# Softmax denominators in four strips of 32 columns instead of two of 64

## The chip, the core and the metric

The kernel runs on one NeuronCore of a Trainium2 chip, a core with five engines that each work through a queue of their own: TensorE (PE, matmuls into PSUM; its weight loads are listed apart as PEld), VectorE (DVE), ScalarE (ACT), GpSimd (POOL) and SyncE (SP, which here only issues DMAs). An instruction that waits holds up what stands behind it in the same queue. The metric is the device time of one execution in microseconds; lower is better.

## What is computed

Attention in which a query sees only the keys of its own cluster, followed by a bilinear feed-forward block. Four batches, 8 heads, 768 tokens, head dimension 64; 512 model columns, 1536 hidden columns; all float32.

```python
q_assign = np.argmax(np.einsum('bhsd,hcd->bhsc', q_n, c_n), axis=-1)
k_assign = np.argmax(np.einsum('bhsd,hcd->bhsc', k_n, c_n), axis=-1)
mask = q_assign[:, :, :, None] == k_assign[:, :, None, :]
scores = np.where(mask, scale * np.matmul(q, k.transpose(0, 1, 3, 2)), -1e9)
attn = np.exp(scores - np.max(scores, axis=-1, keepdims=True))
attn = attn / (np.sum(attn, axis=-1, keepdims=True) + 1e-09)
x = bridge(np.matmul(attn, v))               # (B, H, S, D) -> (B*S, H*D)
out = ((x @ w_a) * (x @ w_b)) @ w_out
```

## The kernel before

The work on attention goes by pairs of heads: 16 pairs (4 per batch), numbered p. The 768 queries of a pair are cut into two halves `hf` of 384 (`HB`), the keys into six blocks `j` of 128. One unit is a pair, a half and a block, and the main loop over `g` takes two units per round, a **group**: six groups a pair (`GPP`, `l` is the group within the pair), 96 in all, and three more to finish.

A group issues, in this order: the scores of its two units, keys on the partitions and queries along the columns (`score`, L539: the one-hot product that does the masking, then q times k), their exponentials on ACT (L548, tile `pt`); the check of earlier inverses on ACT (L643); the additions of the units of the group before into `acc` (`add_up`, L569, DVE and, from pair 4 on, mostly POOL); the weighted sums of the group before (`weigh`, L580, tile `O`, copied to `xT` by ACT at L590 after six blocks); a step of preparing the next pair (`prep_sim`, L358, similarities to the centroids in four strips of 32 columns, at `l` = 1; transposes; one-hot rows); and, once per half, `denominators`. Then come pieces of the feed-forward of the batch before, by a credit of PE columns per group, and the rounding of the feed-forward weights (`round_w`, L275 to L297) that is due. `todo` is a queue of small steps, of the preparation and of `normalize`: one is issued after each feed-forward piece, and what is left at the end of the group is issued at once. All of this is an order written out by hand; every engine's queue follows it.

The softmax is not divided where it is computed. A half's sum over the keys is a sum over partitions, so `denominators` (L593) takes it on PE: a matrix of ones is the stationary operand, and head `a` of the pair lands on partitions 64a to 64a+63 of PSUM, every one of its 64 rows holding the same 384 sums (L603). So the sums stand in the layout in which `xT` has the 64 outputs of that head on its partitions. For pairs 0 to 3 there are two terms, the last block's probabilities and `acc`; later pairs add all blocks into `acc` and have one. ACT copies the sums to SBUF, into the first half of `acc`, and adds them up for a final check (L608).

`normalize` (L612) is four steps. `across` (L623): DVE transposes the sums in blocks of 32x32, so that the 384 sums of a partition stand as 12 elements on each of 32 partitions. `invert` (L626): a reciprocal of those 12 columns instead of 384. `back` (L630): the transpose back, each inverse read 32 times. `apply` (L635): POOL multiplies `xT` by the inverses. Up to group 25 these steps come at `l` = 4 (first half) and `l` = 1, one group after L603; later at `l` = 5 and `l` = 3 (at `l` = 2 after the last group). L603 then stands at `l` = 4 and, right after L358, at `l` = 1.

`acc` has two buffers, one for each half in turn; a half's buffer is written again by the first addition (L569) of the half after next. `ps_m`, from which L342, L358, L603 and the feed-forward take their PSUM tiles, has three buffers, `ps_s` (scores) two, `ps_o` one.

The feed-forward of batch 0 is plain on the way up: four chunks a product (L663), an evacuation by ACT (L674) or a multiplication by DVE (L678) after each. Those of batches 1 to 3 use Strassen-Winograd products: pieces of two chunks (L767) evacuated by DVE additions (L777) and an ACT copy (L791), combinations of inputs and weights on DVE (L723, L735, L750), multiplications on POOL (L782); the way down is L893 (256 columns) with DVE additions (L899) for all batches. A batch's `xT` is complete when its last half is normalized; `combine_x` (L723) reads it then. The last feed-forward runs alone at the end.

Of the kernel before, what the change touches and what calls it, by code (L numbers as in the profile page):

```python
# [8 lines left out]
FP32 = mybir.dt.float32  # L9
# [4 lines left out]
AF = mybir.ActivationFunctionType  # L14
ALU = mybir.AluOpType
# [15 lines left out]
P = 128  # L31
# [105 lines left out]
def short_path(nc, tc, ctx, c, cn, centroids_in, casts, n_far, q, k, v,  # L137
# [3 lines left out]
    B, H, S, D = q.shape  # L141
# [3 lines left out]
    HP = H // 2  # L145
    NPAIR = B * HP
    NCH = DM // P
    NF = DF // P
    HB = S // 2

    def pool(name, bufs, space=None):
        kw = {} if space is None else {"space": space}
        return ctx.enter_context(tc.tile_pool(name=name, bufs=bufs, **kw))
# [9 lines left out]
    small = pool("small", 2)  # L163
# [11 lines left out]
    ident, identb, ones, rank = c["ident"], c["identb"], c["ones"], c["rank"]  # L175
# [10 lines left out]
    def by_blocks(p):  # L186
        return p >= HP
# [164 lines left out]
    def prep_sim(p):  # L352
# [4 lines left out]
        for kq in range(4):  # L357
            nc.tensor.matmul(out=ps[32 * kq:32 * kq + 32, 0:HB],  # L358
                             lhsT=cTb[:, hp, :],
                             rhs=qkTs[p][:, kq * HB:(kq + 1) * HB],  # L360
                             start=True, stop=True)
        if by_blocks(p):
            sims[p] = ps
            return
        t = simp.tile([P, HB], FP32, name="sim")
        nc.scalar.copy(out=t, in_=ps[:, 0:HB])
        sims[p] = t

    def prep_across(p):
        ps = ps_m.tile([P, 512], FP32, name="m")  # L370
        for t in range(3):
            nc.tensor.transpose(out=ps[:, t * P:(t + 1) * P],
                                in_=sims[p][:, t * P:(t + 1) * P],
                                identity=ident)
        return ps
# [52 lines left out]
    def prep_onehot_first(kq):  # L428
# [3 lines left out]
        for n in (3, 4, 5, 0, 1, 2):  # L432
# [3 lines left out]
                                identity=identb)  # L436
        c0 = kq * HB
        nc.scalar.activation(out=ohTs[0][:, S + c0:S + c0 + HB],
                             in_=ps[:, HB:S], func=AF.Identity, scale=FAR,
# [57 lines left out]
    def prep_steps(p):  # L497
        if p >= NPAIR:
            return [lambda: None] * 6

        def both(*fs):
            return lambda: [f() for f in fs]

        if by_blocks(p):
            steps = prep_by_blocks(p)
            ready = [lambda s=s: todo.extend(s) for s in steps]
            ready[1] = both(lambda: prep_sim(p), lambda: load_v(p), ready[1])
            return ready

        return [  # L510
            both(lambda: prep_transpose(p, 0), lambda: prep_transpose(p, 1)),
            both(lambda: prep_sim(p), lambda: load_v(p)),
            lambda: todo.extend(prep_assign(prep_across(p))),
            lambda: None,
            lambda: prep_onehot(p, 1),
            lambda: None,
        ]
# [2 lines left out]
    probs, accs, O_of, den_of, xTs = {}, {}, {}, {}, {}  # L520
    unchecked = []
    todo = deque()
    UPP = 2 * NJ
    NU = NPAIR * UPP

    def where(u):
        p, l = divmod(u, UPP)
        hf, j = divmod(l, NJ)
        return p, hf, j

    def score(us):
        tiles = [ps_s.tile([P, 2, 512], FP32, name="s") for _ in us]

        def add(Ts, start):
            for u, s in zip(us, tiles):
                p, hf, j = where(u)
                for a in range(2):
                    r = slice(a * D, (a + 1) * D)
                    nc.tensor.matmul(  # L539
                        out=s[:, a, 0:HB],  # L540
                        lhsT=Ts[p][r, S + j * P:S + (j + 1) * P],
                        rhs=Ts[p][r, hf * HB:(hf + 1) * HB],
                        start=start, stop=not start)

        def exp():
            for u, s in zip(us, tiles):
                pt = ptp.tile([P, 2, HB], FP32, name="pt")
                nc.scalar.activation(out=pt, in_=s[:, :, 0:HB], func=AF.Exp,  # L548
                                     scale=SCALE)
                probs[u] = pt  # L550

        if us[0] == 0:
            add(qkTs, True)
            return lambda: [add(ohTs, False), exp()]
        add(ohTs, True)
        add(qkTs, False)
        exp()
# [35 lines left out]
    def denominators(p, hf):  # L593


        ps = ps_m.tile([P, 512], FP32, name="m")
        acc = accs.pop((p, hf))
        terms = [acc]
        if p < HP:
            terms.insert(0, probs[p * UPP + hf * NJ + NJ - 1])  # L600
        for n, t in enumerate(terms):
            for a in range(2):
                nc.tensor.matmul(out=ps[a * D:(a + 1) * D, 0:HB], lhsT=ones,  # L603
                                 rhs=t[:, a, :], start=(n == 0),
                                 stop=(n == len(terms) - 1))
        den = acc[:, 0, :]
        n = 4 * p + 2 * hf
        nc.scalar.activation(out=den, in_=ps[:, 0:HB], func=AF.Copy,  # L608
                             accum_out=stat[:, n:n + 1])
        den_of[p, hf] = acc  # L610

    def normalize(p, hf):  # L612

        b, hp = divmod(p, HP)
        acc = den_of.pop((p, hf))
        den, once = acc[:, 0, :], acc[:, 1, :]
        x = xTs[b][:, hp, hf * HB:(hf + 1) * HB]
        inv = small.tile([P, HB // 32], FP32, name="inv")

        def across():
            nc.vector.transpose(out=once, in_=den)  # L623

        def invert():
            nc.vector.reciprocal(  # L626
                out=inv, in_=once.rearrange("p (j t) -> p j t", t=32)[:, :, 0])

        def back():
            nc.vector.transpose(  # L630
                out=den,
                in_=inv[:, :, None].broadcast_to((P, HB // 32, 32)))

        def apply():
            nc.gpsimd.tensor_tensor(out=x, in0=x, in1=den, op=ALU.mult)  # L635
            unchecked.append((4 * p + 2 * hf + 1, inv))

        return [across, invert, back, apply]

    def check_inverses():  # L640
        while unchecked:
            n, inv = unchecked.pop()
            nc.scalar.activation(out=inv, in_=inv, func=AF.Copy,  # L643
                                 accum_out=stat[:, n:n + 1])


    ffn = deque()
# [345 lines left out]

    GPP = UPP // 2
    NG = NPAIR * GPP
# [33 lines left out]
    across = prep_across(0)  # L1029
# [10 lines left out]
    for g in range(NG + 3):  # L1040
        p, l = divmod(g, GPP)
        if l == 0:
            ready = prep_steps(p + 1)
        now = (2 * g, 2 * g + 1)
        before = (2 * g - 2, 2 * g - 1)
        if 0 < g < NG:
            score(now)
        check_inverses()
        if 0 < g <= NG:
            for u in before:  # L1050
                add_up(u)
        flush_w()
        if 0 < g <= NG:
            weigh(before)
        if g < NG:
            ready[l]()
        late = int(g > EARLY)
        if g % 3 == late and 0 < g - late:
            denominators(*divmod(g // 3 - 1, 2))
        parts = due.get(g, [])  # L1060

        def round_next():
            if parts:
                i = parts.pop(0)
                round_w(i)
                load_w(i + 2)

        round_next()
        if g <= EARLY:
            first, second = 4, 1  # L1070
        else:
            first, second = 5, 3 if g < NG else 2
        ph = {first: (p, 0), second: (p - 1, 1)}.get(l)
        halved = ph in den_of
        if halved:
            todo.extend(normalize(*ph))
        if ffn:
            credit += PER_GROUP[(g > 2 * BG + 3) + (g > 3 * BG + 3)]
            least = FREE_ROOM if halved and ph[1] and (ph[0] + 1) % HP == 0 else 0
            while len(ffn) > least and credit > 0:  # L1080
                cost, piece = ffn.popleft()
                credit -= cost
                piece()
                if todo:
                    todo.popleft()()
                round_next()
        else:
            credit = 0
        round_next()
        while todo:  # L1090
            todo.popleft()()
        if halved:
            ffn_ready(*ph)
        if l == 0 and p + 1 < NPAIR:
            if not by_blocks(p + 1):
                prep_transpose(p + 1, 2)
            load(p + 2)
        if l == 4 and p + 1 < NPAIR and not by_blocks(p + 1):
            prep_onehot(p + 1, 0)

    def some_ffn(n):
        for _ in range(n):
# [15 lines left out]
    ps = ps_m.tile([P, 512], FP32, name="m")  # L1118
    nc.tensor.matmul(out=ps[0:1, 0:1], lhsT=far_off, rhs=ones[:, 0:1],
                     start=True, stop=True)  # L1120
# [227 lines left out]
```

## Time and profile before

| | |
|---|---|
| median of 6 runs | 1064.47 us (1064.26 to 1065.45) |
| the profiled execution | 1064.52 us |
| its span, first to last instruction | 1062.8 us |
| mean granted clock of PE | 0.999 |
| L603 on PE | 160 records of 128x384, 0.486 us each as listed |
| L608 on ACT | 32 of 128x384, 0.49 us each |
| L623, L626, L630 on DVE | 32 of each, 0.57, 0.22 and 0.58 us |
| L635 on POOL | 32 of 128x384, 1.00 us each |

A record of PE is one pass; an fp32 matmul leaves two. The end of a record is modelled, its start is not, so records overlap in the list. The stretches of the execution, by the engines' busy time in them:

| us | what runs | PE | DVE | ACT | POOL |
|---|---|---|---|---|---|
| 0 to 17 | start, first pair | 12.95 | 8.76 | 7.14 | 2.25 |
| 17 to 113 | pairs 0 to 3, rounding of weights | 95.81 | 76.35 | 59.23 | 18.13 |
| 113 to 340 | pairs, feed-forward of batch 0 | 225.90 | 174.31 | 72.40 | 101.33 |
| 340 to 882 | pairs, the rest of batch 0, batches 1 and 2 | 540.71 | 339.08 | 113.61 | 208.04 |
| 882 to 1062.8 | feed-forward of batch 3 | 173.96 | 110.42 | 7.68 | 24.22 |

A line of the timeline reads: start, time, engine, line of the kernel, operation, what it writes and reads, size, number of records, and in brackets how long the engine stood idle before it and what released it.

### The profile page before, as it was taken

Reading aid. Unit: us, or ns where it says so; the run is one execution under the profiler, and the core shown is the slowest. Engines: PE = TensorE matmul, PEld = TensorE weight load, DVE = VectorE, ACT = ScalarE, POOL = GpSimd, SP = SyncE. Lnnn points to the kernel's source line nnn. Section 1 sums busy time; section 2 is a strip of 40 time slices with the busy share of each in tenths; the row PEclk is TensorE's granted clock in tenths of the full one; section 3 lists DMA queues with packets and bytes.
Section 4 is the critical chain, followed back from the end, with each engine's and each line's share of the span. In section 5 each row is a group of like instructions: output and inputs, shape, how many; then the busy total and the mean of one; then the engine's idle time right before and its main releaser. Section 6 shows DMA issues by size and latency. Waiting matters only on the chain.

```text
span 1062.8 us, 13065 instructions
## 1 busy us (share of the span) xinstructions
PE 1049.3 (99%) x4756; PEld 605.5 (57%) x4756; DVE 708.9 (67%) x1402; ACT 260.1 (24%) x501; POOL 354.0 (33%) x329
## 2 busy tenths in 40 slices
PE   8999999999999999999999999999999999999997
PEld 5444455554556665454545766555545687555686
DVE  5778877887857447676757736767565846676762
ACT  5665333233322221212222121122122200000000
POOL 1111345454533323443545422444334410222200
PEclk9999999999999999999999999999999999999999
DMA  5334243525120120202020030300000000000001
GB/s 165 96 73 101 84 105 104 124 69 138 62 47 15 41 44 19 40 4 45 4 46 1 25 65 22 48 0 19 1 4 1 11 30 21 0 1 1 0 31 33
DMA packets 120504, 46.18 MB, mean 43 GB/s; under 512 B 106608, under 2 KB 115824, under 8 KB 120432
## 3 DMA queue, kind: packets, MB, share of 16 engines
q1 hardware_dynamic: 120016, 44.85, 17.9%
q8 instruction: 39, 0.64, 0.3%
q10 hardware_dynamic: 416, 0.43, 0.1%
q14 instruction: 33, 0.27, 0.1%
HBM read 37.78 MB, written 6.29 MB: 41 GB/s over the span
## 4 chain that ended last, share of the span: by engine, by line
PE 92%; DVE 5%; issue 1%; POOL 1%; DMA 0%; ACT 0%; DVEq 0%; POOLq 0%
PE m L767 30%; PE m L893 20%; PE s L539 14%; PE O L580 12%; PE m L663 11%; PE m L603 2%; PE m L358 1%; DVE raw L723 1%; PE m L342 0%; DVE raw L750 0%; DVE acc L569 0%; DVE xT L723 0%; POOL xT L635 0%; DVE ha L777 0%; DMA wo_sb<-in_centroids_dram 0%
## 5 line engine op out<-in xcount | busy, mean ns | idle before, releaser
L548 ACT ACTIVATE pt<-s 128x768 f32<-128x768 f32 x192 | 145.4, 809 | 307.4 <-PE s L539 253.9
L569 POOL TENSOR_TENSOR acc<-acc,pt 128x384 f32<-128x384 f32 x144 | 151.8, 1068 | 59.8 <-ACT pt L548 43.5
L782 POOL TENSOR_TENSOR h<-h,ha 128x384 f32<-128x384 f32 x72 | 72.6, 1016 | 236.2 <-DVE ha L777 234.7
L580 PE MATMUL O<-pt,v 128*64 128x384 f32 x768 | 145.1, 499 | 0.0
L539 PE MATMUL s<-qkT 64*128 64x384 f32 x768 | 139.6, 482 | 0.0
L777 DVE TENSOR_TENSOR ha<-ha,m 128x384 f32<-128x384 f32 x126 | 66.9, 546 | 73.1 <-PE m L767 72.3
L777 DVE TENSOR_TENSOR h<-h,m 128x384 f32<-128x384 f32 x126 | 67.2, 548 | 64.3 <-PE m L767 63.5
L569 DVE TENSOR_TENSOR acc<-acc,pt 128x384 f32<-128x384 f32 x96 | 73.8, 794 | 35.9 <-POOL acc L569 35.0
L580 PEld LDWEIGHTS O<-pt,v 128*64 128x64 f32 x768 | 46.6, 136 | 86.4 <-issue 84.8
L539 PEld LDWEIGHTS s<-qkT 64*128 64x128 f32 x768 | 70.5, 187 | 31.4 <-issue 0.2
L893 PE MATMUL m<-wo_sb,h 128*128 128x256 f32 x384 | 87.5, 382 | 0.0
L635 POOL TENSOR_TENSOR xT<-xT,acc 128x384 f32<-128x384 f32 x32 | 32.8, 1025 | 147.9 <-DVE acc L630 121.4
L893 PEld LDWEIGHTS m<-wo_sb,h 128*128 128x128 f32 x384 | 72.1, 190 | 16.0 <-issue 4.2
L767 PE MATMUL m<-raw 128*128 128x384 f32 x192 | 70.4, 489 | 0.9 <-DVE ha L777 0.9
L663 PE MATMUL m<-xT,wa_sb 128*128 128x384 f32 x192 | 67.4, 493 | 0.7 <-POOL xT L635 0.7
L663 PE MATMUL m<-xT,wb_sb 128*128 128x384 f32 x192 | 66.8, 491 | 0.0
L893 PE MATMUL m<-xT,h 128*128 128x256 f32 x288 | 65.4, 382 | 0.1
L893 PEld LDWEIGHTS m<-xT,h 128*128 128x128 f32 x288 | 54.1, 190 | 11.7 <-issue 1.7
L767 PE MATMUL m<-xT,wa_sb 128*128 128x384 f32 x144 | 52.9, 491 | 0.4 <-DVE rest L899 0.4
L767 PE MATMUL m<-xT,wb_sb 128*128 128x384 f32 x144 | 52.8, 490 | 0.0
L767 PE MATMUL m<-xT,size 128*128 128x384 f32 x144 | 52.8, 490 | 0.0
L663 PEld LDWEIGHTS m<-xT,wa_sb 128*128 128x128 f32 x192 | 35.4, 190 | 30.5 <-ACT pt L548 3.6
(164 smaller groups left out, 1445.1 us busy)
## 6 DMA issues: line engine op xcount, KB each, us to landing
raw<-in_moe_w_a_dram SPq DMA_DIRECT2D x12, 512.0 KB, 4.4
raw<-in_moe_w_b_dram SPq DMA_DIRECT2D x12, 512.0 KB, 3.6
raw<-in_moe_w_out_dram SPq DMA_DIRECT2D x12, 512.0 KB, 3.3
qk<-in_q_dram SPq DMA_DIRECT2D x48, 96.0 KB, 3.0
qk<-in_k_dram SPq DMA_DIRECT2D x48, 96.0 KB, 3.6
v<-in_v_dram SPq DMA_DIRECT2D x24, 192.0 KB, 3.9
out_dram<-rest SPq DMA_DIRECT2D x24, 128.0 KB, 1.7
v<-in_v_dram SPq DMA_DIRECT2D x4, 384.0 KB, 4.4
```

Of the source, the lines that this page charges most:

```text
L358: nc.tensor.matmul(out=ps[32 * kq:32 * kq + 32, 0:HB], lhsT=cTb[:, hp, :], rhs=qkTs[p][:, kq * HB:(kq + 1) * HB], start=True, stop=True)
L539: nc.tensor.matmul(out=s[:, a, 0:HB], lhsT=Ts[p][r, S + j * P:S + (j + 1) * P], rhs=Ts[p][r, hf * HB:(hf + 1) * HB], start=start, stop=not ...
L548: nc.scalar.activation(out=pt, in_=s[:, :, 0:HB], func=AF.Exp, scale=SCALE)
L569: eng.tensor_tensor(out=acc[:, a, :], in0=probs[u - 1][:, a, :] if j == 1 else acc[:, a, :], in1=probs[u][:, a, :], op=ALU.add)
L580: nc.tensor.matmul(out=O_of[0][a * D:(a + 1) * D, 0:HB], lhsT=vs[p][:, a, j, :], rhs=probs[u][:, a, :], start=(j == 0), stop=(j == NJ - 1))
L603: nc.tensor.matmul(out=ps[a * D:(a + 1) * D, 0:HB], lhsT=ones, rhs=t[:, a, :], start=(n == 0), stop=(n == len(terms) - 1))
L635: nc.gpsimd.tensor_tensor(out=x, in0=x, in1=den, op=ALU.mult)
L663: nc.tensor.matmul(out=ps[:, 0:HB], lhsT=w_sb[:, ch, f * P:(f + 1) * P], rhs=xTs[b][:, ch, t0:t0 + HB], start=(ch == 0), stop=(ch == NCH - 1))
L767: nc.tensor.matmul(out=ps[:, 0:HB], lhsT=A[l][c], rhs=rhs[c], start=(c == 0), stop=(c == 1))
L777: nc.vector.tensor_tensor(out=out, in0=in0, in1=ps, op=op)
L782: nc.gpsimd.tensor_tensor(out=to, in0=to, in1=box[name], op=ALU.mult)
L893: nc.tensor.matmul(out=ps[:, 0:HN], lhsT=A[l][f // 3][:, f % 3, :], rhs=B[r][f // 2][:, f % 2, :], start=(f == 0), stop=(f == N2 - 1))
```

## The change

A head's 384 queries are cut once more, into two quarters of 192 (`QB`), and the sums are taken in four strips of 32 columns of ones: strip 2a+i holds quarter i of head a on 32 partitions. ACT's copy and the transpose across then have 192 columns, 6 columns of sums to invert. The reciprocal writes them twice, side by side (12 elements). But a head's 64 partitions need the inverses of both its quarters, and each strip has only its own: four copies of 32 partitions by 6 columns (`move`) fetch, for each strip, the inverses of the other strip of its head. ACT does them when feed-forward pieces are waiting at that moment, POOL otherwise. The transpose back and the multiplication keep their sizes.

The steps are also spread. Where feed-forward pieces are waiting, or the pair is one of number 3 or more, an empty step stands between `invert` and `back`. In front of that (pairs 0 to 2), `back` and `apply` are kept in `held` and put on `todo` one group later. The order of the instructions on PE and on SP stays; L603 has twice as many matmuls.

```diff
--- before.py
+++ after.py
@@ -147,6 +147,7 @@
     NCH = DM // P
     NF = DF // P
     HB = S // 2
+    QB = HB // 2
 
     def pool(name, bufs, space=None):
         kw = {} if space is None else {"space": space}
@@ -520,6 +521,7 @@
     probs, accs, O_of, den_of, xTs = {}, {}, {}, {}, {}
     unchecked = []
     todo = deque()
+    held = []
     UPP = 2 * NJ
     NU = NPAIR * UPP
 
@@ -593,6 +595,7 @@
     def denominators(p, hf):
 
 
+
         ps = ps_m.tile([P, 512], FP32, name="m")
         acc = accs.pop((p, hf))
         terms = [acc]
@@ -600,22 +603,25 @@
             terms.insert(0, probs[p * UPP + hf * NJ + NJ - 1])
         for n, t in enumerate(terms):
             for a in range(2):
-                nc.tensor.matmul(out=ps[a * D:(a + 1) * D, 0:HB], lhsT=ones,
-                                 rhs=t[:, a, :], start=(n == 0),
-                                 stop=(n == len(terms) - 1))
-        den = acc[:, 0, :]
+                for i in range(2):
+                    nc.tensor.matmul(out=ps[(2 * a + i) * 32:(2 * a + i + 1) * 32, 0:QB],
+                                     lhsT=ones[:, 0:32],
+                                     rhs=t[:, a, i * QB:(i + 1) * QB],
+                                     start=(n == 0), stop=(n == len(terms) - 1))
+        den = acc[:, 0, 0:QB]
         n = 4 * p + 2 * hf
-        nc.scalar.activation(out=den, in_=ps[:, 0:HB], func=AF.Copy,
+        nc.scalar.activation(out=den, in_=ps[:, 0:QB], func=AF.Copy,
                              accum_out=stat[:, n:n + 1])
         den_of[p, hf] = acc
 
-    def normalize(p, hf):
+    def normalize(p, hf, move):
 
         b, hp = divmod(p, HP)
         acc = den_of.pop((p, hf))
-        den, once = acc[:, 0, :], acc[:, 1, :]
+        den, once, inverse = acc[:, 0, 0:QB], acc[:, 1, 0:QB], acc[:, 0, :]
         x = xTs[b][:, hp, hf * HB:(hf + 1) * HB]
-        inv = small.tile([P, HB // 32], FP32, name="inv")
+        n = QB // 32
+        inv = small.tile([P, 2 * n], FP32, name="inv")
 
 
 
@@ -623,19 +629,27 @@
             nc.vector.transpose(out=once, in_=den)
 
         def invert():
+            column = once.rearrange("p (j t) -> p j t", t=32)[:, :, 0]
             nc.vector.reciprocal(
-                out=inv, in_=once.rearrange("p (j t) -> p j t", t=32)[:, :, 0])
+                out=inv.rearrange("p (i j) -> p i j", i=2),
+                in_=column[:, None, :].broadcast_to((P, 2, n)))
+
+            for r in range(0, P, 32):
+                i = r // 32 % 2
+                other = r + 32 - 64 * i
+                move(out=inv[r:r + 32, (1 - i) * n:(2 - i) * n],
+                     in_=inv[other:other + 32, (1 - i) * n:(2 - i) * n])
 
         def back():
             nc.vector.transpose(
-                out=den,
-                in_=inv[:, :, None].broadcast_to((P, HB // 32, 32)))
+                out=inverse,
+                in_=inv[:, :, None].broadcast_to((P, 2 * n, 32)))
 
         def apply():
-            nc.gpsimd.tensor_tensor(out=x, in0=x, in1=den, op=ALU.mult)
+            nc.gpsimd.tensor_tensor(out=x, in0=x, in1=inverse, op=ALU.mult)
             unchecked.append((4 * p + 2 * hf + 1, inv))
 
-        return [across, invert, back, apply]
+        return [across, invert], [back, apply]
 
     def check_inverses():
         while unchecked:
@@ -1054,6 +1068,8 @@
             weigh(before)
         if g < NG:
             ready[l]()
+        todo.extend(held)
+        held.clear()
         late = int(g > EARLY)
         if g % 3 == late and 0 < g - late:
             denominators(*divmod(g // 3 - 1, 2))
@@ -1073,7 +1089,14 @@
         ph = {first: (p, 0), second: (p - 1, 1)}.get(l)
         halved = ph in den_of
         if halved:
-            todo.extend(normalize(*ph))
+
+            one, other = normalize(*ph, nc.scalar.copy if ffn else
+                                   nc.gpsimd.tensor_copy)
+            todo.extend(one)
+            if ffn or ph[0] >= HP - 1:
+                todo.extend([lambda: None] + other)
+            else:
+                held.extend(other)
         if ffn:
             credit += PER_GROUP[(g > 2 * BG + 3) + (g > 3 * BG + 3)]
             least = FREE_ROOM if halved and ph[1] and (ph[0] + 1) % HP == 0 else 0
```

## The prediction

> **What bounds the kernel now.** I read the page first: engines' busy time, then the chain that ended last.
>
> ```profile
> PE 1049.3 (99%) x4756; PEld 605.5 (57%) x4756; DVE 708.9 (67%) x1402; ACT 260.1 (24%) x501; POOL 354.0 (33%) x329
> PE 92%; DVE 5%; issue 1%; POOL 1%; DMA 0%; ACT 0%; DVEq 0%; POOLq 0%
> ```
>
> TensorE (PE) is busy from end to end and is 92% of the chain; what PE is not busy is 13.5 us in all (1062.8 - 1049.3). So a microsecond of matmul that goes is a microsecond of time, unless another engine is late at that place. The changed matmuls are those of L603. The second reading is PE's timeline, where the distance from one start to the next is what a group really takes (the ends are modelled); a wait of PE is below what a start is later than the pass before it would have it. The first three lines are from 159 to 167 us, the last three from 250 to 255 us.
>
> ```profile
> 163.51 1.51 PE L580 MATMUL O<-pt,v 128*64 128x384 f32 x8
> 164.85 0.81 PE L603 MATMUL m<-acc,ones 128*64 128x384 f32 x4
> 165.60 1.88 PE L663 MATMUL m<-xT,wa_sb 128*128 128x384 f32 x5
> ...
> 252.24 0.87 PE L358 MATMUL m<-qkT,cTb 128*32 128x384 f32 x8
> 253.04 0.87 PE L603 MATMUL m<-acc,ones 128*64 128x384 f32 x4
> 253.83 1.56 PE L663 MATMUL m<-xT,wb_sb 128*128 128x384 f32 x4
> ```
>
> An fp32 matmul leaves two records (two passes). L603 has four: two strips of 64 columns side by side, two passes. From the records' starts: a pass of 384 columns of the moving operand takes 0.322 us (L663, L580), of 256 columns 0.215 (L893), of 128 columns 0.109 (L342): a line, 0.84 ns a column. L358 already runs four strips of 32: its four first passes start 7 ns apart and all eight records take 0.80 us to L603, not four times a pass. A change of shape costs 0.094 us after the last pass, and the first pass of the new shape is longer: by 0.024 (32 columns), 0.051 (64), 0.104 (128).
>
> **The change, part by part.**
>
> *Matmuls.* A term becomes four strips of 192 moving columns; by the line above a pass is 192 x 0.84 = 0.161 us. The bounds are the rows on both sides, 0.109 and 0.215; I take the line since three rows lie on it. The order of matmuls on PE is otherwise unchanged.
> - After L580, one term (13 of the 24 halves of pairs 4 to 15): last L580 pass to L663 was 0.322 + 0.745 = 1.067. Now 0.322 + 0.094 (a change of shape that is new), 0.161 + 0.024, 0.02 for the strips' stagger, 0.161 + 0.094: 0.876. Saved 0.19 x 13 = 2.5.
> - After L358 (10 halves): L358 to L663 was 1.59 (252.24 to 253.83). Both are now strips of 32, so the change between them goes: 0.346 + 0.322 for L358, then 0.161 + 0.161 + 0.02 + 0.094 = 1.10. Saved 0.48 x 10 = 4.8.
> - The last (865.56, between L893): 0.79 to 0.46, 0.3.
> - Pairs 0 to 3 have two terms (probabilities, then acc). At 42.8 and 68.6 both are ready before: 1.44 to 0.78, 0.66 each. At 93.3: 1.39 to 0.88, 0.51. At 29.7, 55.5 and 81.3 PE waits for DVE's last acc addition, so only what follows it shrinks, 0.35 each; likewise at 125.0 (0.33). At 104.8 nothing is kept, since PE later waits for DVE anyway (0.85 us at 115.96, released by POOL L635). Sum 1.32 + 0.51 + 1.05 + 0.33 = 3.2.
>
> The change of shape is the term that speaks against the edit. The trace prices it at 0.094 plus 0.024, already taken 13 times above. The Trainium skill's page "TensorEngine Tiling (Array Packing)", under Key Properties, says that a switch of tiling mode drains the engine and gives no price; by the rule alone one could expect more, by the row 0.12 us a time. Its page "TensorE: Matmul & The Clock Gate", under Measured speedup vs the span model, has three column strips at 2.38 times one, 79% of ideal; as an estimate from that page, 0.161/0.79 would make the time some 3 us longer than I forecast. L358's row shows no such loss at 384 columns; none at 192 is in this trace.
>
> *Vector and scalar work.* L608 and L623 take half the columns. ACT: operations on 768, 512 and 384 columns take 0.81, 0.59 and 0.48, so 192 take about 0.31 (0.17 saved). DVE's transpose of 384 takes 0.57; I take half plus little, 0.30 (0.27 saved). The reciprocal writes 12 elements as before, the transpose back 384. None of it is on PE's path but for the places below.
>
> *Four copies of 32x6.* 25 halves put them on ACT, 7 on POOL. The nearest ACT rows are L643's:
>
> ```profile
> 114.64 0.21 ACT L643 ACTIVATE inv<-inv 128x12 f32<-128x12 f32 x1 [1.97 <-DVE acc L630]
> 114.76 0.19 ACT L643 ACTIVATION_READ_ACCUMULATOR inv<-inv 128x1 f32 x1
> ```
>
> 0.21 each, starts 0.1 apart when they overlap: four take 0.52 to 0.85. On POOL the nearest are a 128x1 memset (0.10) and the 128x128 select (0.29): four take 0.4 to 1.2; I take 0.6 for both. With two handovers (0.04 to 0.1 by the gaps of L643 and L569) the step back, which started 0.034 after the reciprocal, starts 0.7 later: 0.4 net of the shorter transpose.
> Who waits: on ACT the copies wait for DVE's reciprocal, and behind them stand the next exponentials or an evacuation (L674, L791). ACT's exponentials are used one group later, 8 to 10 us away, with 1.6 us of work. On DVE behind L630 stand the next evacuations and acc additions; DVE waits for PE for 72 + 64 us at L777. In 6 halves of pairs 0 to 2 the step back is put off by a group: its cover is that group (4 us), and its acc buffer is first wanted two groups after that. In the feed-forward one more piece lies between (1.3 us for L767's, 2.6 for L663's and L893's), where pieces are left in the group.
> Cover is missing at the end of groups, where the queue is emptied at once. This is 393 to 397 us:
>
> ```profile
> 393.93 0.57 DVE L623 STREAM_TRANSPOSE acc<-acc 128x384 f32<-128x384 f32 x1
> ...
> 394.79 0.58 DVE L630 STREAM_TRANSPOSE acc<-inv 128x384 f32<-128x384 f32 x1
> ...
> 395.52 1.00 POOL L635 TENSOR_TENSOR xT<-xT,acc 128x384 f32<-128x384 f32 x1 [6.90 <-DVE acc L630]
> ...
> 396.55 0.56 DVE L569 TENSOR_TENSOR acc<-pt 128x384 f32<-128x384 f32 x1 [1.18 <-POOL xT L635]
> ...
> 397.03 1.35 DVE L723 TENSOR_TENSOR raw<-xT 128x384 f32<-128x384 f32 x1
> ```
>
> DVE waits for POOL's L635 in 11 such places (13.1 us, by that line's own view). PE then has scores and weighted sums (3.2 us) that need no evacuation, which covers 0.4 more. It doesn't where six L723 subtractions follow: PE waits for DVE at 404.23 and 657.79 already (0.37 each). There the 0.4 goes onto PE, and the 0.19 of that group's L603 is lost: 2 x 0.6 = 1.2. The third such place (880) has slack: L630 ends at 880.6, L723 starts at 887.7.
> At 113.19 the POOL copies lie on the chain that PE waits for at 115.96: +0.7, less two shorter transposes (0.54): +0.2.
>
> **Sum**: 2.5 + 4.8 + 0.3 + 3.2 - 1.2 - 0.2 = 9.4 us. The profiled execution took 1064.52 (span 1062.8, 1.7 around it), as good as the median 1064.47: **1055.2**.
>
> **Rivals.**
> 1. Group ends: the 0.4 reaches PE at all 11 places. For: DVE waits there today. Against: PE shows no wait after nine of them. 11 x 0.4 = 4.4: 1059.6.
> 2. Short passes don't scale: 0.215, as L893's. About 68 passes count (48, and 20 in pairs 0 to 3), 68 x 0.054 = 3.7: 1058.9. For: eight weight loads of 0.106 us have to lie beside 0.37 us. Against: L358's loads of four strips start 7 ns apart.
> 3. Slower: ACT's queue becomes the bound. ACT, which never waited for DVE's normalisation before L643, now does before evacuations; PE has three such buffers. If each of the 25 halves holds PE for the full 0.7 us, that is 17.5 against a gain of 10.6: 1071. It decides from 0.42 us a half. For: DVE's evacuations already come late for PE at 518 and 771 us (0.6 each, L777). Against: in 19 of the 25 halves ACT starts nothing for 0.5 us or more after the reciprocal, and in five of the others it is exponentials.
> 4. The strips don't share time: passes stay at 0.322. Then a half costs 0.13 more 13 times and 0.16 less 10 times (1.7 - 1.6), some 0.8 more in pairs 0 to 3, and the copies 1.0: 1066.4.
>
> **Chances.** Forecast 0.62 (its own range 1053.6 to 1057.0); rival 1 0.13; rival 2 0.12; rival 3 0.07; rival 4 0.03; a gain that is waited away to within 0.2% 0.03. A change of 0.2% (2.1 us) is about what can be told from none. Faster 0.87 (forecast, rivals 1 and 2), same 0.06, slower 0.07. The range takes in rivals 1 and 2, and on the low side passes a little shorter than the line: 1053.0 to 1060.0.
>
> **What will show it.** L603's records 128*32, 128x192; 0.44 to 0.46 us from its start to the next form; 1.10 from L358 to L663. PE's waits unchanged but for 404 and 657 (0.6 instead of 0.37) and 115.96. L630 about 0.7 after L626 where no piece lies between. I am wrong if waits of PE for ACT L674 or L791 appear, or if L603 still takes 0.7.

## The result, and the profile after

The changed kernel takes 1062.31 us (median of 19 runs, 1062.12 to 1063.43), the kernel before, timed beside it, 1065.31 (39 runs, 1064.24 to 1065.92): a ratio of 0.9975, 95% interval 0.9969 to 0.9982. It is faster by 0.25%, 2.7 us by the ratio, where 9.4 were forecast: the sign is right, the size is not, and the time lies outside the range. The profiled execution took 1063.02 us, its span 1061.3.

The executions of a kernel end in two groups about 1 us apart (before 1064.5 and 1065.6, after 1062.25 and 1063.2; the profiled one of after is of the upper group, in which PE's transposes near 8 us start 0.213 us apart, that of before of the lower, with 0.109), so "like for like" below compares the means within one group, by which the change is worth 2.3 us.

The page of after, the lines of busy time and of the chain:

```profile
PE 1042.3 (98%) x4916; PEld 604.1 (57%) x4916; DVE 702.3 (66%) x1402; ACT 275.2 (26%) x601; POOL 365.1 (34%) x357
PE 89%; DVE 7%; issue 1%; POOL 1%; ACT 0%; DMA 0%; DVEq 0%; POOLq 0%; ACTq 0%
```

PE's busy time fell by 7.0 us, but what it is not busy rose from 13.5 to 19.0, and DVE's share of the chain from 5% to 7%. (Part of a wait is listed as busy, since ends are modelled: a kernel with the same matmuls and fewer waits, the first experiment's, lists 1039.5.)

PE's timeline of after, 164 to 167 and 312 to 315 us, the two surroundings of the sums (L607, before L603):

```profile
164.14 1.51 PE L582 MATMUL O<-pt,v 128*64 128x384 f32 x8
165.58 0.53 PE L607 MATMUL m<-acc,ones 128*32 128x192 f32 x8
166.04 1.24 PE L677 MATMUL m<-xT,wa_sb 128*128 128x384 f32 x3
...
312.47 0.85 PE L359 MATMUL m<-qkT,cTb 128*32 128x384 f32 x8
313.13 0.51 PE L607 MATMUL m<-acc,ones 128*32 128x192 f32 x8
313.57 0.59 PE L677 MATMUL m<-xT,wb_sb 128*128 128x384 f32 x1
```

The matmuls do what was worked out: 0.46 from L607 to the next form after L582, 0.44 after L359, and 1.10 from L359 to L677. So the gain is there and must be lost elsewhere. PE's waits in the execution of after (total in us, times, longest):

```profile
PE m L607 <- DVE acc L571: 2.7, 5, 0.8
PE m L781 <- DVE rest L913: 2.0, 2, 1.0
PE m L677 <- POOL xT L649: 1.7, 1, 1.7
...
PE m L359 <- DVE qkT L461: 0.7, 1, 0.7
...
PE m L907 <- DVE raw L881: 0.3, 1, 0.3
```

Of the same waits, before had only these:

```profile
PE m L663 <- POOL xT L635: 0.7, 1, 0.7
...
PE m L603 <- DVE acc L569: 0.4, 1, 0.4
PE m L767 <- DVE rest L899: 0.4, 2, 0.2
```

All are waits for DVE or POOL; none is for ACT's evacuations (L688, L805). Taken from PE's starts, what comes later than the pass before it would have it is: 0.50 and 0.93 at 56 and 58 us, the same at 82 and 84, 1.90 at 117 (0.85 before), 0.23 at 194 and 0.86 at 254 (0.09 of each is the change of shape), 1.18 at 405 and 1.19 at 658 (0.37 each before), 0.64 at 590.

The end of a group, 393 to 398 us of after (with one line of PE behind it), is the stretch that the prediction showed:

```profile
394.52 0.37 DVE L629 STREAM_TRANSPOSE acc<-acc 128x192 f32<-128x192 f32 x1
...
394.92 0.23 DVE L633 RECIPROCAL inv<-acc 128x12 f32<-128x12 f32 x1
395.18 0.81 ACT L640 COPY inv<-inv 32x6 f32<-32x6 f32 x4 [5.89 <-DVE inv L633]
...
396.02 0.58 DVE L644 STREAM_TRANSPOSE acc<-inv 128x384 f32<-128x384 f32 x1 [0.87 <-ACT inv L640]
...
396.75 1.00 POOL L649 TENSOR_TENSOR xT<-xT,acc 128x384 f32<-128x384 f32 x1 [7.54 <-DVE acc L644]
...
397.78 0.56 DVE L571 TENSOR_TENSOR acc<-pt 128x384 f32<-128x384 f32 x1 [1.18 <-POOL xT L649]
...
405.45 1.56 PE L781 MATMUL m<-xT,wa_sb 128*128 128x384 f32 x4 [1.02 <-DVE rest L913]
```

ACT's four copies do not overlap: 0.81 us together, and DVE stands idle 0.87 between the reciprocal and the transpose back, where it went on after 0.03 before.

### The profile page after: what moved, and what is told of

Same layout as the page of the kernel before. It is cut to its first block, busy times and chain, and to the rows that moved or that the text cites. A ratio compares the mean times of both kernels' runs of the same rounds, so it can differ in the third digit from the quotient of the medians.

```text
span 1061.3 us, 13508 instructions
## 1 busy us (share of the span) xinstructions
PE 1042.3 (98%) x4916; PEld 604.1 (57%) x4916; DVE 702.3 (66%) x1402; ACT 275.2 (26%) x601; POOL 365.1 (34%) x357
## 4 chain that ended last, share of the span: by engine, by line
PE 89%; DVE 7%; issue 1%; POOL 1%; ACT 0%; DMA 0%; DVEq 0%; POOLq 0%; ACTq 0%
PE m L781 30%; PE m L907 19%; PE s L541 14%; PE O L582 11%; PE m L677 11%; PE m L359 1%; PE m L607 1%; DVE acc L571 1%; DVE raw L737 1%; PE m L343 1%; DVE raw L764 0%; POOL xT L649 0%; DVE acc L644 0%; DVE xT L737 0%; DVE ha L791 0%
## 5 line engine op out<-in xcount | busy, mean ns | idle before, releaser
L582 PE MATMUL O<-pt,v 128*64 128x384 f32 x768 | 145.1, 499 | 0.0
L571 DVE TENSOR_TENSOR acc<-acc,pt 128x384 f32<-128x384 f32 x96 | 77.5, 833 | 41.5 <-POOL acc L571 39.2
L582 PEld LDWEIGHTS O<-pt,v 128*64 128x64 f32 x768 | 46.6, 136 | 86.4 <-issue 84.8
L649 POOL TENSOR_TENSOR xT<-xT,acc 128x384 f32<-128x384 f32 x32 | 33.1, 1035 | 162.7 <-DVE acc L644 160.4
L907 PE MATMUL m<-wo_sb,h 128*128 128x256 f32 x384 | 87.5, 382 | 0.0
L907 PEld LDWEIGHTS m<-wo_sb,h 128*128 128x128 f32 x384 | 72.1, 190 | 14.6 <-issue 3.6
L781 PE MATMUL m<-raw 128*128 128x384 f32 x192 | 70.4, 489 | 0.9 <-DVE ha L791 0.9
L677 PE MATMUL m<-xT,wa_sb 128*128 128x384 f32 x192 | 67.4, 493 | 1.7 <-POOL xT L649 1.7
L677 PE MATMUL m<-xT,wb_sb 128*128 128x384 f32 x192 | 66.8, 491 | 0.0
L907 PE MATMUL m<-xT,h 128*128 128x256 f32 x288 | 65.4, 382 | 0.1
L907 PEld LDWEIGHTS m<-xT,h 128*128 128x128 f32 x288 | 54.1, 190 | 11.1 <-issue 1.4
L781 PE MATMUL m<-xT,wa_sb 128*128 128x384 f32 x144 | 53.0, 492 | 2.1 <-DVE rest L913 2.0
L781 PE MATMUL m<-xT,size 128*128 128x384 f32 x144 | 52.9, 490 | 0.0
L781 PE MATMUL m<-xT,wb_sb 128*128 128x384 f32 x144 | 52.9, 490 | 0.0
L677 PEld LDWEIGHTS m<-xT,wa_sb 128*128 128x128 f32 x192 | 35.4, 190 | 30.6 <-ACT pt L550 3.6
```

The source lines that it names most:

```text
L571: eng.tensor_tensor(out=acc[:, a, :], in0=probs[u - 1][:, a, :] if j == 1 else acc[:, a, :], in1=probs[u][:, a, :], op=ALU.add)
L582: nc.tensor.matmul(out=O_of[0][a * D:(a + 1) * D, 0:HB], lhsT=vs[p][:, a, j, :], rhs=probs[u][:, a, :], start=(j == 0), stop=(j == NJ - 1))
L649: nc.gpsimd.tensor_tensor(out=x, in0=x, in1=inverse, op=ALU.mult)
L677: nc.tensor.matmul(out=ps[:, 0:HB], lhsT=w_sb[:, ch, f * P:(f + 1) * P], rhs=xTs[b][:, ch, t0:t0 + HB], start=(ch == 0), stop=(ch == NCH - 1))
L781: nc.tensor.matmul(out=ps[:, 0:HB], lhsT=A[l][c], rhs=rhs[c], start=(c == 0), stop=(c == 1))
L907: nc.tensor.matmul(out=ps[:, 0:HN], lhsT=A[l][f // 3][:, f % 3, :], rhs=B[r][f // 2][:, f % 2, :], start=(f == 0), stop=(f == N2 - 1))
```

## The experiments

My theory A was that the strips alone are worth what the working gave them (10.8 us, or 10.6 with the 0.2 at 116 taken off), and that the exchange of inverses (four copies, `held`, the empty step) costs the rest. The rivals: B, that PE, being faster, meets lateness of DVE and POOL that was hidden, so that the loss would come with the strips alone too; and, if A holds, which piece of the exchange costs: the handover to another engine, ACT's queue, or the time itself. "The plain queue" below means that all four steps are put on `todo` at once, as before the change: `todo.extend(one + other)`, without `held` and without the empty step. Diffs are against after unless said.

**Strips without the exchange** (plain queue).

```diff
-            for r in range(0, P, 32):
-                i = r // 32 % 2
-                other = r + 32 - 64 * i
-                move(out=inv[r:r + 32, (1 - i) * n:(2 - i) * n],
-                     in_=inv[other:other + 32, (1 - i) * n:(2 - i) * n])
```

> The strips without the exchange: the four copies are left out, so half of each head's inverses are those of the wrong queries, and the four steps of normalize follow each other as before the change (nothing held, no empty step). Theory A (the matmuls save the 10.6 us worked out, and the exchange gives most of it back, because the transpose back starts 0.87 us after the reciprocal instead of 0.03 and, where it is held, stands in front of the acc additions that PE waits for): 1054 to 1056, with PE's waits at 56, 82, 194 and 254 us gone and those at 405 and 658 near 0.4 instead of 1.2. Theory B (the other engines set the time at those places anyway, so a faster L607 only waits longer): 1060 to 1062.

Measured: 1053.79 us, ratio 0.9896 (0.9881 to 0.9912), a little below the range of A; like for like 10.8 to 10.9 us below before, where the working has 10.8 without its 1.2 and 0.2. PE's waits in its execution (L776 is after's L781, L672 its L677):

```profile
PE m L672 <- POOL xT L644: 0.8, 1, 0.8
...
PE m L607 <- DVE acc L571: 0.6, 1, 0.6
...
PE m L776 <- DVE rest L908: 0.4, 2, 0.2
```

The waits at 56, 82, 194, 254 and 590 us are gone, but for 0.16 at each of the first two. A holds and B falls.

**The exchange without the strips** (two strips of 64; against before).

```diff
             nc.vector.reciprocal(
                 out=inv, in_=once.rearrange("p (j t) -> p j t", t=32)[:, :, 0])
+            n = HB // 64
+            for r in range(0, P, 32):
+                i = r // 32 % 2
+                other = r + 32 - 64 * i
+                move(out=inv[r:r + 32, (1 - i) * n:(2 - i) * n],
+                     in_=inv[other:other + 32, (1 - i) * n:(2 - i) * n])
...
-            todo.extend(normalize(*ph))
+            one, other = normalize(*ph, nc.scalar.copy if ffn else
+                                   nc.gpsimd.tensor_copy)
```

The rest, `held` and the empty step, is as in after.

> The kernel before with its two strips of 64 columns, plus the four copies, the empty step and the held steps of the change; the copies here fetch equal values, so nothing is left out. Theory A: the exchange costs what the change lost, 5 to 8 us over before, with new waits of PE where the changed kernel has them. Theory B: within 2 us of before, since PE has its old length and the other engines their old slack.

Measured: 1073.4 us, ratio 1.0086 (1.0072 to 1.0100), some 8.7 us above before, more than the 5 to 8 expected of A, with waits at the same places as after. The 8.5 us that after lies above the strips alone and these 8.7 are the same loss, whether PE is the faster or the slower one.

**Nothing held in front of the feed-forward.**

```diff
-            if ffn or ph[0] >= HP - 1:
-                todo.extend([lambda: None] + other)
-            else:
-                held.extend(other)
+            todo.extend([lambda: None] + other)
```

> The changed kernel without held: in front of the feed-forward the transpose back and the multiplication follow in the same group as the reciprocal, with POOL's copies as they are. Theory A: the two waits of 0.8 us for acc at 56 and 82 us go, 1.6 us faster than the changed kernel, about 1060.7. Theory B' (the hold is right, because POOL's copies stand behind the weight addition L291 of 1.27 us and DVE would wait for them): no faster than the changed kernel or up to 2 us slower.

Measured: 1061.02 us, ratio 0.9965 (0.9953 to 0.9977): 1.3 us below after. The waits at 56 and 82 go, one of 1.0 at 104 comes, and that at 116 stays at 1.90. So `held` costs something; POOL's copies in the same group cost something too.

**The copies on DVE** (plain queue).

```diff
-            one, other = normalize(*ph, nc.scalar.copy if ffn else
-                                   nc.gpsimd.tensor_copy)
+            one, other = normalize(*ph, nc.vector.tensor_copy)
```

> The changed kernel with the four copies on DVE itself, nothing held, no empty step: no handover between engines. Theory A: the transpose back starts 0.3 to 0.6 us after the reciprocal's end, and DVE has some 0.2 us more work per half than before the change; 1055 to 1058. Theory B: 1060 to 1063.

Measured: 1061.72 us, ratio 0.9972 (0.9963 to 0.9982). That is outside A's 1055 to 1058 and, by its number, in the range of B, which the first two runs had excluded. It is instructive: no engine is handed anything, ACT has no copies, and it costs nearly what after costs. DVE's copies of 32x6 take 0.165 us, 0.175 apart, so the transpose back comes 0.76 us after the reciprocal, nearly as late as with ACT. It comes later still where a copy starts while POOL is in the middle of an instruction: all 16 such copies take 0.27 to 0.94 and end 0.02 after POOL's instruction, while the other 112 take 0.16 to 0.17. So the delay is 1.3 to 1.4 us at 142, 182 and 242. Two of PE's waits in this execution:

```profile
PE m L359 <- DVE qkT L461: 2.6, 2, 1.4
PE m L781 <- DVE rest L913: 1.8, 2, 0.9
```

Neither the handover nor ACT's queue is needed for the loss, then; it is the time that passes on DVE between the reciprocal and what follows.

**Two copies on ACT, two on DVE** (plain queue).

```diff
-                move(out=inv[r:r + 32, (1 - i) * n:(2 - i) * n],
-                     in_=inv[other:other + 32, (1 - i) * n:(2 - i) * n])
+                move[i](out=inv[r:r + 32, (1 - i) * n:(2 - i) * n],
+                        in_=inv[other:other + 32, (1 - i) * n:(2 - i) * n])
...
+            one, other = normalize(*ph, (nc.scalar.copy, nc.vector.tensor_copy))
```

> The changed kernel with two of the four copies on ACT and two on DVE, at the same time, nothing held, no empty step: the transpose back should start 0.45 us after the reciprocal, against 0.87 with ACT alone, 0.76 with DVE alone and 0.03 without copies. If the delay is what costs, in proportion: 1056.5 to 1058.5, between the strips alone (1053.8) and the copies on DVE (1061.7). If it has a threshold that 0.45 us stays under: near 1054. If the handover to another engine costs as such: 1060 or more.

Measured: 1064.37 us, ratio 0.9996 (0.9987 to 1.0005). By its number this is the case in which the handover costs as such (1060 or more); place by place it is not. Beside the feed-forward (groups 24 to 93) it is 1.0 us better than after: where the delay is 0.48 us, PE loses 0.45 at each of 405, 590 and 658 in place of 0.84. At 194 and 254 it loses as much as after or more (1.4 and 1.6), but there DVE's first copy stands beside POOL's L291 again, takes 0.74 to 0.78 at 148, 188 and 247, and the transpose back is 1.1 late. In front of the feed-forward, ACT's copies stand in its queue behind exponentials, and the transpose back comes 2.4 to 4.5 us after the reciprocal:

```profile
PE m L607 <- DVE acc L571: 4.2, 4, 1.5
...
PE s L541 <- ACT pt L550: 1.1, 3, 0.4
```

So what a copy costs is set by what its queue holds at that moment, and in front of the feed-forward ACT was rightly avoided.

**A dose: four, two and no copies beside the feed-forward**, none in front of it (plain queue; `None` for `move` there). Four:

```diff
-            for r in range(0, P, 32):
+            for r in range(0, P, 32) if move else ():
...
+            one, other = normalize(*ph, nc.scalar.copy if ffn else None)
```

> The strips with the four copies on ACT beside the feed-forward only; in front of it they are left out (wrong inverses for half of the queries of those halves), and nothing is held and no empty step put in. By the starts of the score groups the changed kernel loses 5.4 us against the strips alone between group 24 and the end, and 3.2 before. If the loss beside the feed-forward is due to the copies: 1053.8 + 5.4 = 1059.2, within 1. If the empty step has a part in it, 1 us or more to either side.

and two:

```diff
-            for r in range(0, P, 32):
+            for r in range(0, P, 64) if move else ():
```

> As the one with four copies on ACT beside the feed-forward, but with two of the four (the other two left out, so a quarter of the queries get wrong inverses): the transpose back starts 0.46 us after the reciprocal instead of 0.87. If PE's loss is in proportion to the delay: 2.8 us over the strips alone, 1056.6. If the slack of DVE hides the first 0.4 us: 1054 to 1055. If the first handover costs most of it: 1058 or more.

Measured: 1058.67 us (0.9946, 0.9931 to 0.9961) and 1056.89 us (0.9925, 0.9909 to 0.9940). Like for like they lie 4.9 and 2.2 us above the strips alone; the transpose back starts 0.87 and 0.46 us after the reciprocal, against 0.03 (where no piece of the feed-forward lies between). The price follows the delay, nearly in proportion as a whole but not place by place: at 194 two copies cost nothing. Four copies, PE's waits:

```profile
PE m L781 <- DVE rest L913: 2.1, 2, 1.0
...
PE m L359 <- DVE qkT L461: 0.7, 1, 0.7
```

How such delays reach PE at 194 us is read from the slack there. DVE and PE before, then after:

```profile
191.31 1.83 DVE L460 STREAM_TRANSPOSE qkT<-qk 128x768 f32<-128x768 f32 x2
193.74 0.85 PE L358 MATMUL m<-qkT,cTb 128*32 128x384 f32 x8
```

```profile
193.29 1.83 DVE L461 STREAM_TRANSPOSE qkT<-qk 128x768 f32<-128x768 f32 x2
194.31 1.38 PE L359 MATMUL m<-qkT,cTb 128*32 128x384 f32 x6
195.19 0.52 PE L607 MATMUL m<-acc,ones 128*32 128x192 f32 x4
195.52 0.49 PE L359 MATMUL m<-qkT,cTb 128*32 128x384 f32 x2
```

DVE transposes the next pair's q and k in two parts. Before, the first part ended 1.46 us ahead of PE's use (0.89 at 252 us). With the strips alone it is 1.48 and 0.90; with two copies 0.74 and 0.13, less by twice 0.4; with four it is used up, and PE waits, for the second part too (195.52). A pair has two halves, and DVE has not made up for the first one's delay when the second's comes. What it waits for in after, 130 to 194 us:

```profile
DVE acc L571 <- POOL acc L571: 5.5, 3, 2.1
DVE h L692 <- PE m L677: 4.3, 2, 3.7
DVE acc L644 <- ACT inv L640: 1.8, 2, 0.9
```

The waits for PE lie ahead of 145 us; from there to 194 DVE's longer pauses are for POOL and, at 145.7 and 185.3, 0.87 each, for ACT's copies. A wait for PE would take such a delay up, since PE does not come later by it. A wait for POOL does not, where POOL is late by the same step: at 146.36 and 185.93 POOL's L649 starts after 0.73 and 0.78 of idle time that ends with DVE's L644, with the strips alone after none, and its additions stand behind it.

**`held` and the empty step alone, no copies.**

The copies' loop is removed as in the first experiment; in the main loop:

```diff
-            one, other = normalize(*ph, nc.scalar.copy if ffn else
-                                   nc.gpsimd.tensor_copy)
+            one, other = normalize(*ph, None)
             todo.extend(one)
             if ffn or ph[0] >= HP - 1:
                 todo.extend([lambda: None] + other)
             else:
                 held.extend(other)
```

> The changed kernel with held and the empty step as they are and all four copies left out (wrong inverses for half of the queries). If the order made by held is what costs in front of the feed-forward, because DVE does the transpose back directly ahead of the acc additions that PE waits for, with POOL's multiplication beside them: PE's waits at 56 and 82 us stay, 2.4 us over the strips alone, 1056 to 1056.5, and beside the feed-forward nothing. If it is POOL's copies: as the strips alone, 1053.8 within 0.5.

Measured: 1056.28 us, ratio 0.9920 (0.9904 to 0.9937): 2.5 us above the strips alone. By PE's starts, 2.5 are lost at 55 and 81 us (waits of 0.50 and 0.93, twice, less the 0.16 that the strips alone have), and beside the feed-forward the empty step costs 0.3, at 794 us. The mechanism stands in the timeline of after, where the same happens:

```profile
54.85 0.56 DVE L410 TENSOR_TENSOR oh<-sim,first 128x384 bf16<-128x384 f32 x1
...
55.33 0.57 DVE L644 STREAM_TRANSPOSE acc<-inv 128x384 f32<-128x384 f32 x1
...
55.83 1.79 DVE L571 TENSOR_TENSOR acc<-acc,pt 128x384 f32<-128x384 f32 x2
...
56.05 1.15 POOL L649 TENSOR_TENSOR xT<-xT,acc 128x384 f32<-128x384 f32 x1 [7.76 <-DVE acc L644]
...
57.67 0.52 PE L607 MATMUL m<-acc,ones 128*32 128x192 f32 x4 [0.76 <-DVE acc L571]
```

The held transpose now stands directly ahead of the two additions that PE waits for, and POOL's multiplication runs beside the second: the two end 1.79 us after the first starts, where before they took

```profile
55.39 1.02 DVE L569 TENSOR_TENSOR acc<-acc,pt 128x384 f32<-128x384 f32 x2
```

So 0.57 of the transpose and 0.8 of the slower addition fall where there is no cover. A group earlier, where the transpose back stands with the strips alone, DVE is idle for 1.30 us in after (up to 47.2).

**The exchange earlier, on the sums.** If lateness after the reciprocal is the price, the sums can be exchanged before it, a group earlier, when nobody waits; `normalize` is then the one of before, on 384 columns (plain queue). First from PSUM:

```diff
         nc.scalar.activation(out=acc[:, 0, 0:QB], in_=ps[:, 0:QB], func=AF.Copy,
                              accum_out=stat[:, n:n + 1])
+        nc.scalar.copy(out=acc[:, 0, QB:HB], in_=ps[:, 0:QB])
+        for r in range(0, P, 32):
+            i = r // 32 % 2
+            other = r + 32 - 64 * i
+            nc.scalar.copy(out=acc[r:r + 32, 0, (1 - i) * QB:(2 - i) * QB],
+                           in_=ps[other:other + 32, 0:QB])
```

> Four strips, but the exchange is moved to where the sums leave PSUM: ACT writes the 192 columns twice (for a strip's own quarter, whichever it is) and copies the other strip's quarter over one of the two, six operations instead of one, a group before the inverses are wanted; then the transpose, the reciprocal and the transpose back follow each other as before the change, on 384 columns, with nothing held and no empty step. If what cost the time is the delay between the reciprocal and the transpose back on DVE: as good as the strips alone, 1053.5 to 1056 (the transpose is 0.2 us longer than there, ACT has some 1.6 us more per half in a queue that is a quarter busy). If it is the amount of exchange work, or ACT's queue: 1059 or more.

Measured: 1059.11 us, ratio 0.9945 (0.9932 to 0.9959), in the range that was set down for the amount of work or ACT's queue. The PSUM tile is now held for six operations of ACT, and PE waits for it five times:

```profile
PE m L779 <- ACT acc L618: 2.8, 5, 0.6
```

Then PSUM read once, and the five further copies from SBUF to SBUF (against the kernel just told):

```diff
-        nc.scalar.copy(out=acc[:, 0, QB:HB], in_=ps[:, 0:QB])
+        nc.scalar.copy(out=acc[:, 0, QB:HB], in_=acc[:, 0, 0:QB])
...
-            nc.scalar.copy(out=acc[r:r + 32, 0, (1 - i) * QB:(2 - i) * QB],
-                           in_=ps[other:other + 32, 0:QB])
+            cross = slice((1 - i) * QB, (2 - i) * QB)
+            nc.scalar.copy(out=acc[r:r + 32, 0, cross],
+                           in_=acc[other:other + 32, 0, cross])
```

> As the exchange at the PSUM copy, but PSUM is read once: ACT takes the sums to SBUF as in the changed kernel, and the five further copies (the whole, then the four strips) go from SBUF to SBUF, so the PSUM tile is free after the first. The run with the exchange at PSUM had five waits of PE of 0.73 us each for that tile (3.7 us) that the strips alone had not. Theory A (delay on DVE, and in that run the held PSUM tile): 1054 to 1056. If ACT's 1.6 us more per half hold up its evacuations of the feed-forward as such: still 1058 to 1060.

Measured: 1056.89 us, ratio 0.9926 (0.9912 to 0.9940), 0.9 above the range of A; those waits are gone. What it has above the strips alone, 2.1 us, is for 1.2 in front of the feed-forward, where scores wait for ACT's exponentials (0.26 to 0.54, five times). Last, those five copies on POOL in front of the feed-forward, on ACT beside it:

```diff
+        move = nc.scalar.copy if ffn else nc.gpsimd.tensor_copy
+        move(out=acc[:, 0, QB:HB], in_=acc[:, 0, 0:QB])
+        for r in range(0, P, 32):
+            i = r // 32 % 2
+            other = r + 32 - 64 * i
+            cross = slice((1 - i) * QB, (2 - i) * QB)
+            move(out=acc[r:r + 32, 0, cross],
+                 in_=acc[other:other + 32, 0, cross])
```

> The exchange of the sums from SBUF to SBUF, with POOL in place of ACT for the five further copies in front of the feed-forward, where PE waited for ACT's exponentials (1.2 us over the strips alone up to group 24). If POOL's copies (some 0.5 us each) lie beside other work there: 1055.5 to 1056.5. If DVE, which shares time with POOL in the rows where both run (an addition of 0.55 us took 1.35 beside POOL), is slowed: 1057 to 1059, with the wait for acc near 56 and 82 us back.

Measured: 1056.01 us, ratio 0.9918 (0.9901 to 0.9934), which computes all that the reference asks for and is faster than both kernels. Its five copies, of 32 times as many columns as after's four, cost 1.8 us in place of 8.5 like for like, since they stand where their result is not awaited. One wait is longer than with the strips alone:

```profile
PE m L677 <- POOL xT L649: 1.4, 1, 1.4
```

It is the one in front of the first feed-forward (0.8 there). By PE's starts, 0.2 more is lost at each of 399, 584 and 650, as much as DVE's transpose of 384 columns takes longer than that of 192 (0.57 and 0.37), and 0.35 at 889, which was not followed up.

## Why the prediction was wrong

*The matmuls: right.* The terms 2.5, 4.8, 0.3 and 3.2 summed to 10.8; the strips alone give 10.8 to 10.9 like for like and, by PE's starts, 2.3, 4.7, 0.3 and 3.6. In the last one (pairs 0 to 3), 0.4 is kept at 104.8, where nothing was to be kept. A pass of 192 columns takes 0.162 us (0.161 worked out). The loss that the Trainium skill's measured speedup of three column strips ("TensorE: Matmul & The Clock Gate", Measured speedup vs the span model) would have made, an estimated 3 us, does not show.

*The step that failed* is the cover of the copies: "PE then has scores and weighted sums (3.2 us) that need no evacuation, which covers 0.4 more", with a cost at 404 and 657 alone, 1.2, and 0.2 at 116. The exchange costs 8.5 us. By experiment, like for like: 4.9 for ACT's copies beside the feed-forward (the dose), 2.5 for `held` (alone), and 1.1 left over. In after itself, by PE's starts against the strips alone, the loss is 2.5 at 56 and 82, 0.9 at 117 (a wait of 1.90 in place of 0.99, where POOL's copies stand; with `held` alone it does not grow), 5.1 at five places beside the feed-forward and 0.3 at 801 (the empty step), less 0.1 at 104. In its parts:
- *The size of the delay.* Taken as 0.7, less 0.27 for the shorter transpose: 0.4 net. Measured: 0.87 (four copies 0.207 apart, and none overlaps; the pairs of L643 that I had read as overlapping were an operation with its own read of the accumulator), and the transpose of 192 columns takes 0.37 in place of 0.30, so 0.64 net. PE's extra wait at 405 and 658 became 0.8 each, where the forecast charged 0.6 (the 0.4 and the 0.19 lost). Its sign for them, "0.6 instead of 0.37", did not follow from that: 0.37 and 0.6 make 0.97.
- *Cover measured one half at a time.* I asked at each group's end whether PE had 3.2 us to go on with. It does eight times of eleven: besides the two that the prediction names, the end at 587 reaches PE at 590, by way of DVE's L881, which PE's L907 waits for. And DVE's delay stays in its queue: two halves of a pair add 1.7 us, and the slack where PE next needs DVE is 1.48 and 0.90. Against the strips alone, after loses 1.0 at 194, 1.6 at 254 and 0.84 at 590, places that the prediction does not name, which with the 0.8 at 405 and at 658 make 5.1, the 4.9 of the dose within 0.2.
- *Held halves*: "its cover is that group (4 us)" looked only at the time the copies need. The steps put off had to land somewhere, and landed ahead of additions that PE waits for, with POOL's multiplication beside them. A moved step was priced at its old place, not at its new one.

*Rival 1*, lateness at all eleven group ends, was the nearest in kind and gave 1059.6; but only three of those ends reach PE (at 405, 590 and 658), with 0.8 each and not 0.4, and the larger losses at 194 and 254 are delays of two halves that add up. "A gain that is waited away to within 0.2%" came nearest to the time; it had a chance of 0.03 and no working. *Rivals 2 and 4* (short passes, strips that don't share time) fall by L607's starts. *Rival 3*, ACT's queue, falls: in after PE never waits for L688 or L805, and with the copies on DVE the loss stays.

*What was to show it*: the matmul signs came as said (0.46, 0.44, 1.10). "PE's waits unchanged but for 404 and 657 and 115.96" did not: there are waits at 56, 82, 194, 254 and 590 besides, and the three that it names are longer than forecast.

## What to carry to other kernels

On an engine that is busy from end to end, matmul time falls as the distances between starts say, so the arithmetic can be trusted; whether it is kept is decided by the others. An engine that is busy two thirds of the time can still have only a microsecond of slack at the places where it is needed: measure that slack, from the end of its result to its use, and set against it the sum of all delays since the two last met, not one of them. Extra steps cost least where their result is used latest; the same exchange cost 8.5 us between the reciprocal and its use, and 1.8 one group ahead of it.

## What the runs showed of the hardware

- Copies of 32x6: ACT 0.195 us each, 0.207 apart; DVE 0.165, 0.175 apart; POOL 0.18, 0.22 apart (up to 0.61 beside DVE). DVE's transpose takes 0.37 for 192 columns and 0.57 for 384.
- Strips of different instructions run side by side: at 195 us L607's first two strips run while L359's other strips wait (above). The Trainium skill's page "TensorEngine Tiling (Array Packing)", under Key Properties, says that tiles operate independently; this trace agrees. And no change of shape is paid between the two lines: at 312 L607 starts 0.66 us after L359, twice 0.322 and the stagger.
- Some operations of DVE wait POOL out. With the copies on DVE, each of the 16 that start while POOL is in an instruction ends 0.02 us after that instruction, up to 0.94 us long in place of 0.165. An addition on DVE beside POOL's multiplication took 1.36 us; of the 52 additions into `acc` of after with no POOL work beside them, none took over 0.56.
